# Score products of the gated attention as four 64x64 tiles, placed ahead of the preceding unit's outputs, with other PSUM banks for the outputs

## The chip, the core and the metric

The kernel runs on one core of a Trainium2 chip. TensorE (PE in the profile, PEld for its weight loads) does the matrix products and writes them to PSUM, VectorE (DVE) and ScalarE (ACT) work elementwise and read PSUM, GpSimd (POOL) works elementwise on SBUF, SyncE (SP) issues the DMA transfers. The metric is the device time of one launch in microseconds; lower is better.

## The reference, cut to what matters

Three stages run one after the other on a sequence of 4 batches x 768 steps x 384 columns: a gated linear attention of 8 heads of 48, a two-layer MLP behind a layer norm, and a token-mixing block followed by a second MLP.

```python
f = 1.0 / (1.0 + np.exp(-f_logit))
for t in range(S):                       # per batch b and head h, state is 48 x 48
    state = f[:, :, t, :, None] * state + np.einsum('bhd,bhe->bhde', k[:, :, t], v[:, :, t])
    y[:, :, t] = np.einsum('bhd,bhde->bhe', q[:, :, t], state)
...
xn = (x - mu) / np.sqrt(var + 1e-06) * g_ln
x = x + np.maximum(xn @ w_ch1, 0.0) @ w_ch2
...
u = x + (np.maximum(x.transpose(0, 2, 1) @ w_tok1, 0.0) @ w_tok2).transpose(0, 2, 1)
out = u + np.maximum(u @ w_ch1, 0.0) @ w_ch2
```

## The kernel before

**Units of attention.** The recurrence is cut into chunks of 128 steps. A unit n is one chunk of one batch with all 8 heads: 24 units, unit n being chunk n // 4 of batch n % 4. Heads lie in 4 pairs p, and the two heads r of a pair stand in two halves of the partitions (rows 0 to 47 and 64 to 111). The logarithms of the gates are summed along the chunk, and queries and keys are scaled with the exponentials, so that a chunk becomes plain products. Each step of a unit has a name, used in the order table as `unit.step`:

- `lf`, `lq`, `lv` (or `lt`, `lv` from unit 3 on): loads of the gate logits, of queries and keys, of values; from unit 3 one load `lt` brings logits, queries and keys as one tile `T` (two buffers)
- `clamp` (VectorE or GpSimd), `log` (two ScalarE activations), `scan` (VectorE), `ek` and `eq` (ScalarE exponentials), `km` and `qm` (keys and queries scaled), `tot` (GpSimd)
- `kp`, `kt`: 4 transposes of the keys on TensorE and their copy out of PSUM
- `sc` (line 318): the scores, 8 products of 48 rows x 128 columns with a stream of 128; `A0`, `A1` (line 323) mask them and copy them to SBUF
- `y`: the outputs, first state times queries (line 335, 48 rows x 64 or 48 columns; not for the first chunk), then values times scores (line 339, 128 rows x 64 or 48 columns); `yc0`, `yc1` copy them out
- `st` (line 364): keys times values, the addition to the state; `ste` adds it, `std` decays it
- `yt` (4 transposes), `lna`, `lnc`, `lnv`, `lnr` (layer norm), `tp` (3 transposes), `ah`, `al` (the normed rows split into two parts for three-product matmuls)

An fp32 product on TensorE appears in the trace as two passes, so 8 products are 16 records.

**MLP work.** Behind the attention, three units make one step of the first MLP: 12 groups `mS.f` (line 469) and 12 groups `mS.ouG` (line 499) of 9 matmuls of 384 columns each; `h`, `l`, `r` are their copies out of PSUM. `wI.ld/.a/.b/.c/.h/.l` load and convert one piece of weights for them. Token mixing and the second MLP follow.

**What sets the order.** Every step is put on a slot list. Up to slot 77 the order of all engines is the table `ORDER`, written out by hand; `name+k` puts k filler products (`busy`, line 432, bf16 zeros of 256 columns) ahead of that step's own products. 56 such products (line 572) also open the program. Behind slot 77 the order follows the slot numbers of the tuple at the end of `attention`: with `s0` the unit's base slot and 8 slots to a unit, one slot being a group of 9 MLP matmuls, `sc` stands at s0-1, `y` and `st` at s0+2, `yt` at s0+4, `kp` at s0-3, `tp` at s0+7. Engines work strictly in this order.

**PSUM.** `mmp` has 3 banks for the MLP, `scp` 2 banks that scores and outputs `yT` take in turn, `atp` 3 banks for `kp`, `y`, `st` and `tp` in turn.

The function that the change touches, with the lines that the profile names:

Of the kernel before, what the change touches and what calls it, by code (L numbers as in the profile page):

```python
# [7 lines left out]
F32 = mybir.dt.float32  # L8
# [13 lines left out]
C = 128  # L22
# [29 lines left out]
    1.tot 0.y+6 1.qm 2.log 2.lq 3.clamp 1.km 0.yc0 0.yc1 2.scan 1.kp+7 3.log 2.lv 1.sc w5.ld w2.a 2.ek
    3.scan 0.yt 2.eq w15.ld 1.kt 2.km 3.ek 1.st+8 w14.ld 1.A1 0.std 3.eq 2.kp 1.A0 0.lna 4.lt 2.qm 1.y+4
    1.ste 2.kt 0.lnc 1.yc0 3.qm 0.tp+3 1.yc1 2.st 0.ah 3.lv 3.km 1.yt 0.lnv 0.al 1.std 3.sc w1.ld 1.lna w2.b
    w4.ld 3.kp 2.ste 1.lnc 3.kt 3.A1 4.lv 4.clamp 1.tp+3 3.st 3.A0 1.ah w12.ld 0.lnr 1.lnv 1.al 3.y 4.log
    w1.a w3.ld 2.tot w1.b 3.yc0 5.lv 4.scan 3.yc1 3.ste 2.sc+9 w5.a 4.ek 3.tot 3.yt 4.eq 2.A1 3.std 5.lt
    3.lna 2.A0 4.km 2.y+7 w5.b 4.kp 2.yc0 4.qm 2.yc1 4.kt 2.yt+4 w5.c 4.sc 3.lnc 2.lna w13.ld w2.c w5.h 3.tp
    2.lnc w2.h 4.st 4.A0 5.clamp 3.ah 2.tp 3.lnv 4.A1 w2.l 2.ah 3.al 4.y+5 5.log 2.al 3.lnr 4.tot 2.lnv m0.0
    5.scan 6.lt 4.yc0 4.yc1 w3.a 5.ek 4.yt 4.ste 2.lnr m0.2 4.lna 5.km 6.lv 5.eq 4.lnc 5.kp 5.qm 4.tp 5.kt
    w3.b 5.sc 4.ah 4.lnv 4.std 4.al 5.st 5.A0 5.tot 1.lnr 5.A1 w3.c 5.y+6 6.clamp w3.h w5.l 6.log w1.c m0.5  # L60
    7.lt 5.ste w3.l 5.yc0 5.yc1 m0.h0 6.scan 5.yt m0.h2 5.lna m0.l2 5.std 7.lv m0.l0 6.ek 5.lnc m0.3+12 6.eq
# [5 lines left out]
    w17.b w17.c w11.ld w20.a w17.h m0.o20 w20.b 8.lv w17.l w6.a m0.o11 8.clamp w6.b 8.log w6.c m0.o21 w11.a
    w6.h w11.b m0.r11 w6.l 6.ste m1.o10 w11.c 8.scan w11.h m0.o01 w11.l w20.c m1.o11 7.clamp w21.ld w20.h
    m0.r01 6.std 7.log m0.r21 w22.ld w20.l m1.o00 7.scan m1.o20 w9.a 7.ek w9.b 8.ek m1.r11 7.km 7.eq m1.o01
    8.eq w9.c 8.km w7.ld w9.h 6.tp m0.6 m1.r01 6.lnv 7.tot w10.ld 8.tot 8.qm w8.ld m1.o21 7.qm 6.lnr 7.sc  # L70
    w7.a m0.h6 m1.r21 w9.l m0.l6 m1.6 w7.b w7.c 7.A1 w7.h m1.9 m1.h6 w7.l m1.l6 w10.a m1.7 w10.b m1.h9 w10.c
    m1.l9 w10.h m0.7 m1.h7 w10.l m1.l7 w22.a m1.10 w22.b m0.h7 w22.c w21.a w22.h w21.b 7.kp m1.h10 m0.11
    w22.l 7.kt w21.c 7.A0 w18.ld w21.h 7.st m0.h11 m1.l10 w21.l 7.y m0.l7 w19.ld w8.a w8.b w23.ld m0.9 w8.c
    7.yc0 9.lt 7.yc1 w18.a w8.h w18.b m0.l11 w8.l 8.sc m0.h9 7.ste w18.c m1.8 8.A1 7.std w18.h 9.lv 8.A0
    s0.ld w18.l m0.8 m1.h8 m1.l8 9.clamp m0.l9 8.y w19.a 9.log w19.b s1.ld w19.c m0.h8 m1.11 9.scan w19.h
    m0.l8 w19.l 9.ek m0.10 9.eq w23.a s2.ld m1.h11 9.qm m1.l11 m0.o22 6.ah m0.h10 w23.b 6.al 9.km m0.o12
# [78 lines left out]
def main_path(ctx, tc, qkf_t, v_n, g_rep, w1, w2, wt1, wt2, w3, w4, out, x1_d, f_d):  # L155
# [17 lines left out]
    zeros = const.tile([128, 256], BF16, name="zeros")  # L173
# [66 lines left out]
    def attention(n):  # L240
# [7 lines left out]
        def load(f, rows, name):  # L248
            def g():
                if "T" not in t:  # L250
                    if n < 3:
                        t["T"] = first[:P2, 12 * n:12 * n + 12, :].rearrange("p (j a) c -> p j a c", j=3)
                    else:
                        t["T"] = sb.tile([P2, 3, NP, C], F32, tag="T", name="T")
                nc.sync.dma_start(out=t["T"][:, rows], in_=qkf_t[n][:, rows])  # L255
            sl.e(f, g, name)
# [49 lines left out]
        def ktrans_e():  # L306
            t["kt"] = s1.tile([128, NP * P2], F32, tag="kt", name="kt")
# [63 lines left out]
        def stat_e():  # L371
            new = t["st"][:P2, :NP * D]
# [612 lines left out]
```

## Time and profile before

| | us |
|---|---|
| time before, median of 3 runs (798.78 to 801.06) | 800.78 |
| the profiled execution, its own time | 798.34 |
| the span of that execution, first to last instruction | 796.6 |
| TensorE busy | 785.7 (99%) |
| VectorE busy | 398.5 (50%) |
| ScalarE busy | 332.3 (42%) |
| GpSimd busy | 208.9 (26%) |

The rest of this document sets its sums against the profiled execution, 798.34 us, of which 1.7 us lie outside the span. Its views are read thus: the page gives shares of busy time; the chain names the work that ended last; the waits name which engine stood still for which; a timeline lists instructions of one engine with their start. TensorE overlaps its instructions, so the lengths of its records add up to more than the time that they take; what a stretch of TensorE costs is read from the starts.

### The profile page before, as it was taken

The page shows a single profiled execution, that of the slowest core. Times are in us where ns is not written, and L with a number is a line of the kernel's source. Part 1 is how long each engine was busy: PE and PEld are TensorE (multiplying, and loading weights), DVE is VectorE, ACT ScalarE, POOL GpSimd, SP SyncE. Part 2 cuts the span into 40 slices and gives each one's busy share as a digit, 9 for nine tenths or more (in the row PEclk, how much of TensorE's full clock was granted, in tenths as well). Part 3 has the DMA queues.
Part 4 walks back from the last instruction along what each step waited for, and adds up shares of the span by engine and source line. Part 5 has one row for each costly group of instructions (what it writes and reads, how often), then busy time and mean ns, then how long its engine had stood idle before and what let it go on. Part 6 is the DMA issues. An engine that isn't in the chain of part 4 may idle for free.

```text
span 796.6 us, 14109 instructions
## 1 busy us (share of the span) xinstructions
PE 785.7 (99%) x5618; PEld 758.5 (95%) x5618; DVE 398.5 (50%) x745; ACT 332.3 (42%) x841; POOL 208.9 (26%) x267
## 2 busy tenths in 40 slices
PE   9999999999999999999999999999999999999996
PEld 7799999999999999999999999999999999999996
DVE  6789895554655545555263353525344443434220
ACT  6764453443534425343253453425344444425020
POOL 2552241432423443232004451211211111111000
PEclk9999999999999999999999999999999999999999
DMA  9736353445544345441243553334333433322001
GB/s 252 226 91 199 87 161 99 126 123 158 162 118 147 110 124 175 129 153 51 77 132 90 181 153 104 88 101 130 109 78 101 125 104 104 96 90 60 31 1 34
DMA packets 42844, 93.23 MB, mean 117 GB/s; under 512 B 4800, under 2 KB 25408, under 8 KB 42768
## 3 DMA queue, kind: packets, MB, share of 16 engines
q1 hardware_dynamic: 42768, 92.23, 39.3%
q8 instruction: 46, 0.75, 0.4%
q14 instruction: 30, 0.25, 0.1%
HBM read 76.48 MB, written 15.73 MB: 116 GB/s over the span
## 4 chain that ended last, share of the span: by engine, by line
PE 93%; DMA 3%; DVE 1%; SPq 1%; ACT 1%; issue 0%; POOL 0%; DVEq 0%
PE mo L499 38%; PE mm L469 37%; PE ht L684 3%; PE rt L660 3%; PE sc L318 3%; DMA T<-in_qkf_t 3%; PE yT L339 3%; PE tp L438 2%; PE yT L335 1%; PE y L353 1%; PE st L364 1%; PE kp L303 1%; DMA xr<-x_d 1%; SPq L255 0%; POOL T L267 0%
## 5 line engine op out<-in xcount | busy, mean ns | idle before, releaser
L469 PE MATMUL mm<-ah,w1h 128*128 128x384 f32 x576 | 197.5, 343 | 0.0
L499 PE MATMUL mo<-w2h,hh 128*128 128x384 f32 x576 | 196.8, 342 | 0.0
L469 PE MATMUL mm<-ah,w1l 128*128 128x384 f32 x576 | 192.9, 335 | 0.0
L499 PE MATMUL mo<-w2h,hl 128*128 128x384 f32 x576 | 192.9, 335 | 0.0
L469 PE MATMUL mm<-al,w1h 128*128 128x384 f32 x576 | 192.6, 334 | 0.0
L499 PE MATMUL mo<-w2l,hh 128*128 128x384 f32 x576 | 192.6, 334 | 0.0
L484 ACT ACTIVATE hh<-mm 128x384 fp32r<-128x384 f32 x192 | 94.0, 490 | 206.9 <-PE mm L469 204.2
L488 DVE SCALAR_TENSOR_TENSOR hl<-mm,hh 128x384 fp32r<-128x384 f32 x192 | 106.3, 555 | 139.6 <-ACT hh L484 139.4
L469 PEld LDWEIGHTS mm<-ah,w1h 128*128 128x128 f32 x576 | 108.2, 188 | 2.2 <-issue 0.7
L499 PEld LDWEIGHTS mo<-w2h,hh 128*128 128x128 f32 x576 | 108.1, 188 | 2.0 <-issue 0.5
L469 PEld LDWEIGHTS mm<-al,w1h 128*128 128x128 f32 x576 | 108.3, 188 | 0.0
L499 PEld LDWEIGHTS mo<-w2l,hh 128*128 128x128 f32 x576 | 108.2, 188 | 0.0
L499 PEld LDWEIGHTS mo<-w2h,hl 128*128 128x128 f32 x576 | 108.1, 188 | 0.0
L469 PEld LDWEIGHTS mm<-ah,w1l 128*128 128x128 f32 x576 | 108.1, 188 | 0.0
L738 POOL TENSOR_TENSOR cs<-cs 128x384 f32<-128x384 f32 x56 | 47.4, 848 | 222.5 <-DVE cs L735 183.3
L267 POOL TENSOR_SCALAR T<-T 112x512 f32<-112x512 f32 x17 | 26.1, 1536 | 109.6 <-DMA T<-in_qkf_t 106.6
L451 ACT ACTIVATE ah<-tp 128x384 fp32r<-128x384 f32 x48 | 23.4, 487 | 69.6 <-PE tp L438 69.5
L529 DVE TENSOR_TENSOR xr<-mo,xr 128x384 f32<-128x384 f32 x24 | 13.4, 556 | 67.9 <-PE mo L499 67.9
L518 DVE SCALAR_TENSOR_TENSOR x<-mo,rs,x 128x384 f32<-128x384 f32 x30 | 18.4, 617 | 51.9 <-PE mo L499 51.8
L455 DVE TENSOR_TENSOR al<-tp,ah 128x384 fp32r<-128x384 f32 x48 | 26.4, 551 | 33.1 <-ACT ah L451 33.0
L741 ACT ACTIVATE cs<-cs 128x384 f32<-128x384 f32 x56 | 31.0, 553 | 9.4 <-POOL cs L738 9.3
L323 DVE TENSOR_TENSOR A<-sc,upper 128x512 f32<-128x512 f32 x48 | 31.0, 685 | 7.4 <-PE sc L318 7.2
(142 smaller groups left out, 1015.5 us busy)
## 6 DMA issues: line engine op xcount, KB each, us to landing
cs<-in_w SPq DMA_DIRECT2D x48, 384.0 KB, 3.3
sg<-in_w SPq DMA_DIRECT2D x44, 384.0 KB, 3.9
T<-in_qkf_t SPq DMA_DIRECT2D x21, 672.0 KB, 5.3
f_d<-cu SPq DMA_DIRECT2D x32, 192.0 KB, 1.9
wf<-f_d SPq DMA_DIRECT2D x32, 192.0 KB, 2.5
x_d<-x SPq DMA_DIRECT2D x24, 192.0 KB, 1.9
xr<-x_d SPq DMA_DIRECT2D x24, 192.0 KB, 3.4
out<-xr SPq DMA_DIRECT2D x24, 192.0 KB, 1.9
```

The lines of the kernel that those rows point to most:

```text
L267: eng("clamp").tensor_scalar(f, f, -43.0, None, op0=ALU.max)
L318: nc.tensor.matmul(t["sc"][r][:, p], t["K"][rows(r), p, :], t["Q"][rows(r), p, :])
L323: nc.vector.tensor_tensor(a, t["sc"][g], upper.rearrange("p (o c) -> p o c", o=1).to_broadcast([128, NP, 128]), op=ALU.mult)
L339: nc.tensor.matmul(t["yT"][r][o, p // 2], t["V"][:, D * h:D * h + o.stop - o.start], t["A", r][:, p, :], start=(c == 0 and p < 2), stop=(p ...
L455: nc.vector.tensor_tensor(al, src, ah.bitcast(F32), op=ALU.subtract)
L469: nc.tensor.matmul(ps, w[:, f, k, :], x[:, k, :], start=(i == 0), stop=(i == 8))
L484: nc.scalar.activation(out=hid(f)[0], in_=t[f], func=AF.Relu)
L488: nc.vector.scalar_tensor_tensor(hl, t[f], 0.0, hh.bitcast(F32), op0=ALU.max, op1=ALU.subtract)
L499: nc.tensor.matmul(ps, x, w[:, f, :], start=(f == lo and i == 0), stop=(f == hi and i == 2))
L660: nc.tensor.matmul(t["r"][j][:, :DM], w[:, s, js], t[x, s], start=(s == 0 and i == 0), stop=(s == NCH - 1 and i == 2))
L738: nc.gpsimd.tensor_tensor(t["u"], t["u"], t["h"], op=ALU.subtract)
L741: nc.scalar.activation(out=t["u"], in_=t["u"], func=AF.Abs, accum_out=wlow[:, i:i + 1])
```

## The change

- A score product is issued as two, each with 64 of the 128 key columns: 16 products of 48 rows x 64 columns instead of 8 of 48 x 128. The stream stays 128 long, the results land in the same places.
- In the slot tuple `sc` goes from s0-1 to s0-6.1, just ahead of the `y` of the unit before (s0+2 there); the steps that prepare it go earlier by 2.5 to 5 slots, and the masks `A0`, `A1` by 5.
- The outputs `yT` move from `scp` to `atp`; scores have `scp` alone. `st` has no bank of its own any more: its products go to columns 256 to 447 of the first `yT` bank, beside the outputs in columns 0 to 255.
- The load is split for all units: logits in a tile `F` of their own (s0-16), queries and keys in `T` (s0-13). `kt` has two buffers.
- Filler products have 224 columns instead of 256.
- The table `ORDER` is written anew, with other fillers (89 before, 88 now) and other steps on GpSimd.

TensorE in the middle of the attention, before (`tp` are transposes of unit 12's norm, `sc` the scores of unit 13, `mm` the MLP):

```order
L469 MATMUL mm<-ah,w1h 128x384
L469 MATMUL mm<-al,w1h 128x384
L469 MATMUL mm<-ah,w1l 128x384
L438 MATMUL tp<-ident,xn 128x128 x3
L318 MATMUL sc<-T 128x128 x8
```

and now, where `sc` are the scores of unit 14 and the `yT` rows the outputs of unit 13:

```order
L471 MATMUL mm<-ah,w1h 128x384
L471 MATMUL mm<-al,w1h 128x384
L471 MATMUL mm<-ah,w1l 128x384
L321 MATMUL sc<-T 64x128 x16
L339 MATMUL yT<-T,state_119 64x128 x2
L339 MATMUL yT<-T,state_119 48x128 x2
L339 MATMUL yT<-T,state_119 64x128 x2
L339 MATMUL yT<-T,state_119 48x128 x2
L343 MATMUL yT<-A_2599,V 64x128
```

The scores stood alone behind the transposes, with 27 MLP matmuls between them and the outputs; now the next unit's scores and this unit's outputs are one block.

SyncE's queue of loads at the start, before (`first` and `firstv` hold the first three units, 512 columns are logits, 1024 queries and keys, 1536 all three; `in_w` are weights):

```order
L547 DMA gln<-in_g_rep 128x384
L255 DMA first<-in_qkf_t 112x512
L192 DMA firstv<-in_w 128x768
L255 DMA first<-in_qkf_t 112x512
L255 DMA first<-in_qkf_t 112x1024
L255 DMA first<-in_qkf_t 112x512
L263 DMA firstv<-in_v_n 128x384
L255 DMA first<-in_qkf_t 112x1024
L255 DMA T<-in_qkf_t 112x1536
L192 DMA firstv<-in_w 128x768
```

and now:

```order
L549 DMA gln<-in_g_rep 128x384
L251 DMA first<-in_qkf_t 112x512 x2
L259 DMA first<-in_qkf_t 112x1024 x2
L266 DMA firstv<-in_v_n 128x384 x2
L251 DMA first<-in_qkf_t 112x512
L251 DMA F<-in_qkf_t 112x512
L259 DMA first<-in_qkf_t 112x1024
L266 DMA firstv<-in_v_n 128x384
L193 DMA sg<-in_w 128x768
L193 DMA firstv<-in_w 128x768
```

The first weights went from third place to behind the loads of three units.

The core of the diff (the shift of the preparing steps, and of the table a line):

```diff
-    0.lf w0.ld 1.lf 0.lq 0.clamp 0.log w0.a w0.b 2.lf 0.scan 0.lv 1.clamp 0.ek 1.lq w0.c 0.eq 0.km w0.h
+    0.lf 1.lf 1.lq 0.clamp 0.log 0.lq 1.clamp 1.log 0.scan 0.lv 1.scan 0.ek 1.lv 0.eq 2.lf 1.ek 0.tot 0.qm
...
-    zeros = const.tile([128, 256], BF16, name="zeros")
+    zeros = const.tile([128, 224], BF16, name="zeros")
...
-            t["kt"] = s1.tile([128, NP * P2], F32, tag="kt", name="kt")
+            t["kt"] = s2.tile([128, NP * P2], F32, tag="kt", name="kt")
...
-                    nc.tensor.matmul(t["sc"][r][:, p], t["K"][rows(r), p, :], t["Q"][rows(r), p, :])
+                    for s in (slice(0, 64), slice(64, 128)):
+                        nc.tensor.matmul(t["sc"][r][s, p], t["K"][rows(r), p, s], t["Q"][rows(r), p, :])
...
-            t["yT"] = [scp.tile([128, NP, 128], F32, tag="sc", name="yT") for _ in range(2)]
+            t["yT"] = [atp.tile([128, NP, 128], F32, tag="at", name="yT") for _ in range(2)]
...
-        def stat(z=0):
-            ps = atp.tile([128, 512], F32, tag="at", name="st")
-            t["st"] = ps
-            busy(ps, z)
+        def stat():
+            ps = t["st"] = t["yT"][0].rearrange("p a c -> p (a c)")[:, 256:256 + NP * D]
...
-            load(s0 - 11, slice(0, 3), f"{n}.lt")
-            sl.e(s0 - 11, load_v, f"{n}.lv")
+            lo = (s0 - 16, s0 - 13, s0 - 11)
...
-                (-9, sl.e, pre_clamp, "clamp"), (-8, sl.e, pre_log, "log"), (-7, sl.e, pre_sum, "scan"),
-                (-6, sl.e, pre_ek, "ek"), (-6, sl.e, pre_eq, "eq"), (-5, sl.e, pre_qm, "qm"),
-                (-5, sl.e, pre_km, "km"), (-5, sl.e, pre_tot, "tot"), (-3, sl.p, None if last else ktrans, "kp"),
-                (-2, sl.e, None if last else ktrans_e, "kt"), (-1, sl.p, scores, "sc"),
-                (0, sl.e, lambda: scores_e(0), "A0"), (0, sl.e, lambda: scores_e(1), "A1"),
+                (-13, sl.e, pre_clamp, "clamp"), (-12, sl.e, pre_log, "log"), (-11, sl.e, pre_sum, "scan"),
+                (-10, sl.e, pre_ek, "ek"), (-10, sl.e, pre_eq, "eq"), (-7.5, sl.e, pre_qm, "qm"),
+                (-8.5, sl.e, pre_km, "km"), (-9, sl.e, pre_tot, "tot"), (-3, sl.p, None if last else ktrans, "kp"),
+                (-2, sl.e, None if last else ktrans_e, "kt"), (-6.1, sl.p, scores, "sc"),
+                (-5, sl.e, lambda: scores_e(0), "A0"), (-5, sl.e, lambda: scores_e(1), "A1"),
...
-            nc.tensor.matmul(ps[:, :256], zeros[:, :128], zeros)
+            nc.tensor.matmul(ps[:, :224], zeros[:, :128], zeros)
```

## Rows read from the trace of the kernel before

**Rows 1.** The page: span, and each engine's busy time, share, instructions.

```profile
span 796.6 us, 14109 instructions
PE 785.7 (99%) x5618; PEld 758.5 (95%) x5618; DVE 398.5 (50%) x745; ACT 332.3 (42%) x841; POOL 208.9 (26%) x267
```

**Rows 2.** The chain that ended last: shares by line, and one late piece (start, length).

```profile
PE mo L499 38%; PE mm L469 37%; PE ht L684 3%; PE rt L660 3%; PE sc L318 3%; DMA T<-in_qkf_t 3%; PE yT L339 3%; PE tp L438 2%; PE yT L335 1%; PE y L353 1%; PE st L364 1%; PE kp L303 1%; DMA xr<-x_d 1%; SPq L255 0%; POOL T L267 0%
714.46 18.72 PE mm L469 x108
```

**Rows 3.** Waits of TensorE: waiting <- waited for: us in total, times, longest.

```profile
PE warm L572 <- DVE zeros L542: 1.1, 1, 1.1
PE sc L432 <- ACT ys L345: 1.0, 1, 1.0
PE yT L432 <- DVE A L323: 0.7, 3, 0.3
PE st L364 <- DMA V<-in_v_n: 0.4, 1, 0.4
```

**Rows 4.** Timeline of TensorE, scores between MLP matmuls: start, length, what, passes.

```profile
59.63 0.34 PE L469 MATMUL mm<-ah,w1l 128*128 128x384 f32 x1
59.90 1.16 PE L318 MATMUL sc<-T 48*128 48x128 f32 x16
60.99 0.45 PE L469 MATMUL mm<-ah,w1h 128*128 128x384 f32 x1
61.27 0.34 PE L469 MATMUL mm<-al,w1h 128*128 128x384 f32 x1
```

**Rows 5.** The same view, a block of key transposes, outputs and state products.

```profile
65.61 0.34 PE L469 MATMUL mm<-ah,w1l 128*128 128x384 f32 x1
65.78 0.55 PE L303 MATMUL kp<-ident,T 112*128 112x112 f32 x4
66.26 0.65 PE L335 MATMUL yT<-T,state 48*64 48x128 f32 x16
66.85 1.09 PE L339 MATMUL yT<-A,V 128*64 128x128 f32 x16
67.76 0.62 PE L364 MATMUL st<-V,kt 128*48 128x48 f32 x16
68.31 0.45 PE L469 MATMUL mm<-ah,w1h 128*128 128x384 f32 x1
68.60 0.34 PE L469 MATMUL mm<-al,w1h 128*128 128x384 f32 x1
```

**Rows 6.** Groups by form: weight loads of the state product, count | busy, mean ns.

```profile
L335 PEld LDWEIGHTS yT<-T,state 48*64 48x64 f32 x160 | 8.2, 132 | 4.6 <-issue 2.9 <-DVE hl L488 0.8 <-DVE cu L211 0.2
L335 PEld LDWEIGHTS yT<-T,state 48*48 48x48 f32 x160 | 7.7, 119 | 0.0
```

**Rows 7.** Timeline of TensorE at the start: opening fillers, later fillers, first MLP matmul.

```profile
1.12 8.42 PE L572 MATMUL warm<-zeros 128*128 128x256 bf16 x56 [1.12 <-DVE zeros L542]
9.38 0.82 PE L432 MATMUL kp<-zeros 128*128 128x256 bf16 x6
...
18.61 1.04 PE L432 MATMUL st<-zeros 128*128 128x256 bf16 x8
19.58 0.67 PE L364 MATMUL st<-firstv,kt 128*64 128x48 f32 x16
...
40.72 0.45 PE L469 MATMUL mm<-ah,w1h 128*128 128x384 f32 x1
```

**Rows 8.** Timeline of VectorE at the start, around the first scan.

```profile
6.71 0.36 DVE L201 TENSOR_SCALAR cu<-firstv 128x384 int32<-128x384 int32 x1 [2.27 <-DMA firstv<-in_w]
7.58 1.22 DVE L276 TENSOR_TENSOR_SCAN first<-seg,first 112x512 f32<-112x512 f32 x1
```

**Rows 9.** Busy time by stretch: PE, PEld, DVE, ACT, POOL (counts), clock, DMA.

```profile
0.00:40.70 40.70, 37.44 (x431) 29.95 (x431) 29.39 (x53) 28.30 (x66) 17.72 (x33) 1.00 0.81 234
53.10:86.90 33.80, 33.80 (x246) 32.97 (x244) 31.46 (x65) 16.63 (x37) 8.62 (x12) 1.00 0.49 144
```

**Rows 10.** Waits, all engines: the clamp for its load.

```profile
POOL T L267 <- DMA T<-in_qkf_t: 106.6, 16, 12.6
```

More of the change, by code (lines that the diff above doesn't have):

```diff
@@ L52 @@
[L52 to L61, printed above, removed]
@@ L67 @@
[L67 to L76, printed above, removed]
@@ new lines @@
+    1.eq 3.lf 0.km 2.lq 1.qm 0.kp+17 0.sc 0.kt 1.km 2.clamp 1.kp 0.A1 2.lv 2.log 3.clamp 0.A0 w5.ld 1.tot
+    1.kt 0.y+8 2.scan 3.log w0.ld 0.st 3.lq 1.sc 0.yc0 3.scan 0.ste 0.yc1 2.ek 0.yt 1.A1 0.std 2.eq 4.lf
+    2.km 0.lna w14.ld 2.qm 2.kp+8 2.kt 0.lnc 4.lq 3.ek 1.A0 2.tot 0.tp+6 0.ah w0.a 1.y 4.clamp 3.eq 0.al
+    0.lnv w15.ld 3.qm 1.st 1.yc0 2.sc w0.b w13.ld 1.yc1 1.ste 3.km 4.log 1.yt 2.A1 w4.ld 2.A0 1.std 3.kp+4
+    1.lna 3.lv 3.sc 4.scan 3.kt w3.ld 2.y 1.lnc 4.ek w1.ld 3.A1 0.lnr 1.tp 2.yc0 4.lv 2.st 4.km 1.ah 2.yc1
@@ new lines @@
+    w2.ld 1.al 3.tot 4.eq w0.c 2.ste 5.lf 4.qm w0.h 2.yt+11 1.lnv w1.a 4.kp w3.a 2.lna 3.A0 2.std 4.tot 4.kt
+    4.sc+6 2.lnc 6.lf w3.b 2.tp 4.A1 w0.l 3.y 2.ah 2.lnv 2.al 5.clamp 4.A0 3.st 5.lq 3.yc0 m0.0 3.ste w3.c
+    3.yc1 w2.a w3.h 3.std 5.log 5.lv 3.yt w3.l 4.y w2.b 3.lna 5.scan 4.st 4.yc0 6.lq 3.lnc m0.3 4.yc1 w1.b
+    5.ek 4.ste 1.lnr 5.eq 6.lv 5.km 3.tp 4.yt 3.ah 5.qm 5.kp 4.lna w1.c 5.sc 3.al 5.kt 5.tot 4.lnc 7.lf w1.h
+    3.lnv 5.A1 4.std 4.tp+4 5.A0 w1.l 4.ah 4.lnv 4.al 5.y+6 w14.a w2.c 6.clamp m0.h0 w15.a 5.st 5.yc0 7.lq
@@ new lines @@
+    m1.h4 w17.a w16.h w17.b m1.l4 w16.l m0.o00 w17.c w7.a w17.h m0.o10 w17.l w7.b m0.o21 w7.c w10.a w6.ld
+    w7.h w7.l m0.o01 w8.ld m0.r21 6.scan w19.ld m0.o11 m0.r01 6.ek w6.a 6.eq w6.b m1.o00 6.qm m0.r11 w6.c
+    m1.o10 w8.a w6.h w8.b w6.l m1.o01 w8.c 6.km w8.h m1.o20 m1.r01 6.tot 8.lf w8.l w10.b 6.kp m1.o21 w10.c
+    6.kt 7.scan w11.ld w10.h 6.sc w23.ld m1.r21 8.clamp 7.ek 7.eq m1.o11 w18.ld 6.A1 7.km 8.log 6.A0 w9.ld
+    w10.l 7.kp m1.r11 7.tot m0.6 7.kt 9.lf 8.scan w18.a 8.ek m1.10 w18.b 8.eq w18.c m0.h6 7.qm m0.7 w18.h
@@ new lines @@
+    w20.b m0.l9 8.sc w20.c m1.h9 6.al w20.h m1.l9 s3.ld 7.y w20.l 8.A1 8.A0 m0.o22 10.clamp 9.lq 7.yc0
+    9.scan 7.yc1 10.log m0.o12 w21.a 9.ek w21.b w21.c 9.eq s0.a w21.h m0.o02 9.tot 9.km 11.lf w21.l 9.kp
+    s1.a m0.o03 9.qm m0.o13 m0.r03 s1.b m0.d0 s1.c m0.o23 m0.r13 s0.b m0.d1 s0.c 7.st m0.r23 s0.h 9.sc 9.kt
+    7.ste 10.scan 9.lv 8.y m0.d2 9.A1 7.std 10.ek 9.A0 10.eq 10.lq 8.st 10.tot m1.o12 8.ste 8.std 10.lv 7.yt
+    m1.o22 7.lna 8.yc0 10.km 8.yc1 m1.o13 7.lnc 10.qm 8.yt m1.r13 7.tp 8.lna m1.o02 m1.d1 7.ah 8.lnc 7.lnv
@@ L246, in eng, with load_f, load_q @@
             return nc.gpsimd if n >= P["NV"] or f"{n}.{x}" in POOL else nc.vector
[L248 to L256, printed above, removed]
+        def load_f():
+            t["F"] = first[:P2, 12 * n + 8:12 * n + 12, :] if n < 3 else sb.tile([P2, NP, C], F32, tag="F", name="F")
+            nc.sync.dma_start(out=t["F"], in_=qkf_t[n][:, 2])
+        def load_q():
+            if n < 3:
+                q = first[:P2, 12 * n:12 * n + 8, :].rearrange("p (j a) c -> p j a c", j=2)
+            else:
+                q = sb.tile([P2, 2, NP, C], F32, tag="T", name="T")
+            t["Q"], t["K"] = q[:, 0], q[:, 1]
+            nc.sync.dma_start(out=q, in_=qkf_t[n][:, 0:2])
         def load_v():
@@ L371, in stat_e @@
         def stat_e():
-            new = t["st"][:P2, :NP * D]
+            new = t["st"][:P2]
             if c:
@@ L571, in warm @@
         for _ in range(k):
[L572 removed]
+            nc.tensor.matmul(wt[0][:, :224], zeros[:, :128], zeros)
     sl.p(0.1, lambda: warm(P["WARM0"]))
```

46 lines of the change are left out of this document (23 added, 23 removed).

## The prediction

> **What bounds the kernel now.** First the page's busy times and the chain. TensorE is busy 785.7 of 796.6 us, every other engine half of the span or less [rows 1], and the chain is TensorE nearly throughout: MLP products 75%, scores 3%, outputs 3 + 1% [rows 2]. Then the waits of TensorE: 1.1 us at the very start, 1.0, 0.7 and 0.4 us later [rows 3], the last of these before the MLP runs steadily. So the time is the sum of TensorE's own work, and an edit counts by what it takes out of that sum; work saved elsewhere counts only at the start, where TensorE is kept going with fillers. Then the timelines, for the price of a block. A stretch of 108 MLP matmuls lasts 18.72 us [rows 2], 0.173 each. What a block between MLP matmuls costs is the time from the last matmul ahead of it to the second behind it, less two times 0.173: for scores alone 61.27 - 59.63 - 0.35 = 1.29 us [rows 4]; for key transposes, outputs and state products together 68.60 - 65.61 - 0.35 = 2.64 us [rows 5].
>
> **Reading the blocks.** The transposes take 66.26 - 65.78 = 0.48 until the state product starts, 0.10 of it the pause that scores show too (59.63 + 0.17 to 59.90) [rows 4, 5], so 0.39 is theirs and 2.25 is left for outputs and state products. A unit thus pays 1.29 + 2.25 = 3.54 us for scores, outputs and state products, in two blocks, and the transposes 0.4 a block. The scores use the array in two halves by rows: 16 passes in 8 rounds of two, 60.99 - 59.90 = 1.09 us with the pause at the end. The state product, 48 rows x 64 columns, is the row nearest to the new scores: 16 passes in 66.85 - 66.26 = 0.59 us, pause included [rows 5]. With four passes at a time that is 4 rounds. The values product behind it takes 8 rounds of two without a pause at its end: 0.91 us, 0.114 a round.
>
> **The scores (the largest term).** Split, they are 32 passes instead of 16, in four quarters: 8 rounds again. The split by itself gains nothing; alone between MLP matmuls the new scores cost about what the old ones do. The gain is the place. Directly ahead of the state product, which has the same tile shape, they need no pause between them and no entry and exit of their own: the block grows by 8 rounds and the 1.29 us go. Price of a round: 0.114 by the values product; 0.125 by the difference of old scores and state product (1.09 - 0.59 over 4 rounds). I take 0.114, the row without a pause in it: 0.91 us. Per unit 1.29 - 0.91 = 0.38 saved, 0.29 by the other price. By the order of the changed kernel 16 of the 24 units have their scores directly ahead of a preceding unit's outputs behind the first MLP matmul (unit 8 on); one more has them so ahead of it, units 5 to 7 stand apart and stay as they were. 16 x 0.38 = **-6.1 us** (bounds -4.6 and, if a round is 0.1, -7.8). All of it lies on the path, since TensorE doesn't wait there.
>
> **The start.** The first MLP matmul comes at 40.72 us [rows 7]; of the 39.6 us from the first filler on, the opening fillers take 9.38 - 1.12 = 8.26, 71 later fillers 0.97 / 8 = 0.121 each, 8.6, waits 2.0 [rows 3, 7] and so attention blocks 20.7. The new order has one unit fewer ahead of the first MLP matmul: 2.25 + 0.4 + 0.3 (outputs and state, one block of 4 and one of 3 transposes) move behind it, 2.95. One score block there loses its pauses: 20.7 - 2.95 - 0.4 = 17.3. Fillers, an estimate from these rows by their columns: 56 at 224 / 256 of 8.26, 7.2, and 60 at 0.106, 6.4 (bounds: unchanged per filler, 8.26 and 7.3). That is 1.1 + 7.2 + 6.4 + 17.3 = 32.0 us plus waits. Can the data be there? The first scan stands at 7.58 behind two steps of weights, for which VectorE waited 2.27 us [rows 8]; with these loads and steps moved back it needs only the logarithms, which follow the clamp, and that chain starts nearly 2 us earlier. VectorE has 39 steps ahead of the first MLP matmul instead of 46, some 3.3 us less by their mean times, 26 of its 29.4 us [rows 9]. 26 in 33.5 is 78%, against 72% now and 93% between 53 and 87 us, where TensorE never waited [rows 9]. So I put waits at 1.5 us (before: 2.0; bounds 0, and 8.7, which is no gain at all): first MLP matmul at 33.5, 7.2 earlier, less the 2.95 moved: **-4.3 us** (bounds -5.8 to +3).
>
> **Behind it.** 28 fillers at 0.106 instead of 18 at 0.121 and 0.3 of small waits between them: 3.0 against 2.5, **+0.5**. Another **+0.5** for waits of the new order there that no row shows: VectorE's work up to the second half of the first MLP step is the same with TensorE some 8 us earlier, but below the 93%.
>
> **Edits that I cost at nothing, and what hides them.** The outputs' new banks: `atp` now carries five tiles a unit (two of outputs, two of transposes, one of the norm) on three banks; the key transposes take over the first outputs' bank after 27 MLP matmuls, 4.7 us, while two output copies and the state addition need about 1 us. Without that cover each unit would pay up to 1 us. The state products in the outputs' bank: at worst `yc0` must wait until they end, 0.55 us later [rows 5], covered by 18 MLP matmuls (3.1 us) ahead of the `yt` transposes; at the start, where that cover is short, up to 4 x 0.55, within the waits above. The masks wait for scores in another place of VectorE's queue, and behind them stand the copies of MLP results; since the scores now open a block of over 3 us, these run while TensorE is still in it. The loads: logits come 3 slots ahead of their clamp instead of 2, good for a clamp that waits for its load in 16 units [rows 10]; queries and keys come 6.9 slots ahead of the scores instead of 10, and their buffer is free only once the outputs two units back are done. A slot is 1.56 us of matmuls and its share of blocks, so 6.9 are over 12 us for a load, two scalings and queueing. 21 more DMA issues stand on SyncE, which has room; ahead of them in its queue are weights that aren't due for long.
>
> **The sum.** -6.1 - 4.3 + 0.5 + 0.5 = -9.4 us. The profiled execution took 798.34, so it would take 788.9; the median of the runs is 2.4 above that execution, and from it the sum gives 791.4. I write 791.
>
> **Rivals.** First, the start doesn't shorten: what was filler becomes wait, since the chain of one unit (scores, mask, outputs, copy, transposes, norm) is as long as before. For it: fillers were there because TensorE waits for data, and a shorter filler brings no data. Against it: weights leave that chain. The 4.3 us go: -5.1, about 795.5. Second, the change doesn't do what it says: a pause stays between scores and state product, or scores wait for the scaled queries, whose lead is shorter. For it: clamps already wait for their loads [rows 10]. The 6.1 us go: -3.3, about 797.5; both together leave it where it is, about 801. Third, slower: the four quarters don't load their weights together, and the two that share rows take turns. One score load of 64 columns takes 0.132 us [rows 6]; 16 for each half of the rows in turn are 2.1 us in place of 0.91, +1.2 in 24 units, +28.8 - 9.4, about 820; it decides from 0.4 us a unit, a third of that. Against it: the state product's 16 loads, 8 of 0.132 and 8 of 0.119, 2.0 us together, lie in 0.59 us [rows 5, 6], where turns within each half of the rows would need 1.0.
>
> This third way is also a rule: the Trainium skill ("TensorE: Matmul & The Clock Gate", Part 3, "The mechanism") says that a weight load overlaps running matmuls only when its row group differs. By that rule the sum would be the third rival's; the rows of the state product speak against it, so I give it little.
>
> **How the numbers follow.** Forecast 0.62, start not shortened 0.20, no gain from the block 0.07, both 0.06, loads in turn 0.05. The forecast's own range is 787 (round at 0.1, no waits) to 794; the first two rivals reach to 797, and 786.5 to 797 leaves out about 0.2. A measurement of this kernel can tell about 0.3%, 2.4 us, from no change. Faster by more than that: 0.62 + 0.20 + half of the second rival, 0.86; the same 0.08; slower 0.06.
>
> **What would show it.** In the changed kernel's timeline, 32 passes of scores directly ahead of the state product, the start of one to the start of the other 0.9 to 1.0 us, and a block with state products at 3.1 to 3.2 us where 2.25 stands now; the first MLP matmul at 32 to 35 us; waits of TensorE under 4 us in all. The prediction is wrong if that start is near 40, if TensorE waits for GpSimd or a load at the scores, or if scores take 1.5 us or more.

## The result and the profile after

The changed kernel takes 792.3 us (median; 790.29 to 795.12) against 799.74 (798.78 to 801.06) before: a ratio of 0.9907, interval 0.9881 to 0.9932, or 7.4 us less. On another occasion it took 791.23 against 799.95, ratio 0.9896, interval 0.9876 to 0.9916. The forecast was 791, faster, with a range from 786.5 to 797: direction and time held. The profiled execution took 792.3 us with a span of 790.6; before, 798.34 and 796.6 [rows 1].

The page of the profile after: span, busy time of each engine (share, instructions), and the chain that ended last, by engine and by line (the lines here are those of the changed kernel: scores L321, state product L339, values product L343, state update L366).

```profile
span 790.6 us, 14897 instructions
PE 777.5 (98%) x6001; PEld 756.2 (96%) x6001; DVE 403.9 (51%) x742; ACT 328.8 (42%) x841; POOL 209.6 (27%) x270
PE 90%; DMA 4%; DVE 1%; ACT 1%; POOL 1%; SPq 1%; issue 1%; POOLq 0%; DVEq 0%
```

TensorE has 8.2 us less work and 777.5 of 790.6 us busy; it is still the bound. The 4% of DMA in the chain are for the most part these pieces of it (start, us, what; in order of time), one in the opening and two that end in waits of the first MLP steps:

```profile
4.77 9.53 DMA F<-in_qkf_t
...
99.38 5.00 DMA T<-in_qkf_t
113.63 4.78 DMA T<-in_qkf_t
```

TensorE's waits in the changed kernel, the list that answers to [rows 3]: releaser, us in total, times, longest.

```profile
PE kp L305 <- DVE first L291: 1.8, 2, 1.4
PE sc L321 <- DVE A L326: 1.1, 1, 1.1
PE warm L574 <- DVE zeros L544: 1.1, 1, 1.1
PE kp L305 <- POOL T L291: 1.0, 2, 0.7
PE tp L440 <- DVE xn L394: 0.7, 1, 0.7
```

Without the first filler's these rows are 4.6 us, more than the 4 that the prediction allowed for all waits. The first row holds the 1.44 us of unit 0's keys, the second is a mask that stands behind two weight conversions in VectorE's queue. Next, TensorE's timeline around one block far from the start (start, us, line, operation, count); it answers to [rows 4] and [rows 5].

```profile
138.18 0.34 PE L501 MATMUL mo<-w2h,hl 128*128 128x384 f32 x1
138.45 1.10 PE L321 MATMUL sc<-T 48*64 48x128 f32 x32
139.37 0.62 PE L339 MATMUL yT<-T,state 48*64 48x128 f32 x16
139.92 1.09 PE L343 MATMUL yT<-A,V 128*64 128x128 f32 x16
140.83 0.62 PE L366 MATMUL yT<-V,kt 128*48 128x48 f32 x16
141.38 0.44 PE L501 MATMUL mo<-w2h,hh 128*128 128x384 f32 x1
141.66 0.34 PE L501 MATMUL mo<-w2l,hh 128*128 128x384 f32 x1
```

The 32 quarter passes stand directly ahead of the state product: 139.37 - 138.45 = 0.92 us from the start of one to the start of the other, where the prediction had worked out 0.91. The whole block costs 141.66 - 138.18 - 0.35 = 3.13 us; before, the same products cost 1.29 + 2.25 = 3.54 in two blocks [rows 4, 5]. Eleven units have this block at 3.13, one has it behind another piece, and four, without state update, have 2.69 in place of 3.09.

And the opening, which answers to [rows 7] and [rows 8]: TensorE's first rows, two of those with a wait in them and the first MLP matmul; then VectorE's first scaling of queries.

```profile
1.10 8.10 PE L574 MATMUL warm<-zeros 128*128 128x224 bf16 x56 [1.10 <-DVE zeros L544]
9.04 1.79 PE L434 MATMUL kp<-zeros 128*128 128x224 bf16 x17
12.27 0.57 PE L305 MATMUL kp<-ident,first 112*128 112x112 f32 x4 [1.44 <-DVE first L291]
...
25.27 0.60 PE L305 MATMUL kp<-ident,T 112*128 112x112 f32 x4 [0.33 <-POOL T L291]
...
36.27 0.44 PE L471 MATMUL mm<-ah,w1h 128*128 128x384 f32 x1
```

```profile
10.88 0.69 DVE L294 TENSOR_TENSOR first<-first,eq 112x512 f32<-112x512 f32 x1 [2.00 <-DMA first<-in_qkf_t]
```

The first MLP matmul is at 36.27, not at 33.5. Unit 0's queries are scaled at 10.88, after 2.00 us of waiting for their load; its key transposes, the first work of TensorE that isn't filler, wait 1.44 us behind that.

### The profile page after: what moved, and what is told of

Its sections match the earlier page's. It is cut to its first block, busy times and chain, and to the rows that moved or that the text cites. A ratio compares the mean times of both kernels' runs of the same rounds, so it can differ in the third digit from the quotient of the medians.

```text
span 790.6 us, 14897 instructions
## 1 busy us (share of the span) xinstructions
PE 777.5 (98%) x6001; PEld 756.2 (96%) x6001; DVE 403.9 (51%) x742; ACT 328.8 (42%) x841; POOL 209.6 (27%) x270
## 4 chain that ended last, share of the span: by engine, by line
PE 90%; DMA 4%; DVE 1%; ACT 1%; POOL 1%; SPq 1%; issue 1%; POOLq 0%; DVEq 0%
PE mo L501 38%; PE mm L471 35%; PE ht L686 3%; PE rt L662 3%; PE sc L321 3%; PE yT L343 3%; PE tp L440 2%; DMA T<-in_qkf_t 1%; DMA F<-in_qkf_t 1%; PE yT L339 1%; DMA wf<-f_d 1%; PE yT L366 1%; PE y L357 1%; PE kp L305 1%; DMA xr<-x_d 0%
## 5 line engine op out<-in xcount | busy, mean ns | idle before, releaser
L349 ACT ACTIVATE ys<-yT 112x256 f32<-112x256 f32 x48 | 16.8, 382 | 74.9 <-PE yT L366 55.8
L270 POOL TENSOR_SCALAR F<-F 112x512 f32<-112x512 f32 x19 | 29.9, 1574 | 21.5 <-DMA F<-in_qkf_t 21.5
```

## The experiments

**The scores whole again, in the new place (e1_whole).**

```diff
-                    for s in (slice(0, 64), slice(64, 128)):
-                        nc.tensor.matmul(t["sc"][r][s, p], t["K"][rows(r), p, s], t["Q"][rows(r), p, :])
+                    nc.tensor.matmul(t["sc"][r][:, p], t["K"][rows(r), p, :], t["Q"][rows(r), p, :])
```

> The changed kernel with each head pair's scores as one product over all 128 columns again, in the new place and with the outputs in the other banks. The changed kernel's block of scores, state product, values product and state update costs 3.13 us beyond the MLP matmuls around it. Theory (the gain is that the quarters, half as wide in the array, run side by side with the products behind them, without the pause at a change of tile shape): 3.3 to 3.4 us, over 16 units +3.5 to +4.5 us, total 796 to 797. Rival (the place alone is the gain, one block in place of two): 3.13 as now, total 792. Second rival (the quarters' passes are themselves cheaper): more than 3.5, total 798 or above.

TensorE's timeline of the same block:

```profile
136.56 1.16 PE L320 MATMUL sc<-T 48*128 48x128 f32 x16
137.65 0.65 PE L338 MATMUL yT<-T,state 48*64 48x128 f32 x16
138.23 1.09 PE L342 MATMUL yT<-A,V 128*64 128x128 f32 x16
139.15 0.62 PE L365 MATMUL yT<-V,kt 128*48 128x48 f32 x16
139.70 0.44 PE L500 MATMUL mo<-w2h,hh 128*128 128x384 f32 x1
```

From scores to state product 137.65 - 136.56 = 1.09 instead of 0.92, and the block costs 3.34 instead of 3.13: the pause at the change of tile shape is there again, 0.2 us as the theory said. The total is 793.86 us (ratio 0.9925, 0.9894 to 0.9957), 1.6 to 2.6 us over the two medians of the changed kernel and less than the theory's 796 to 797. The 16 units by 0.21 are 3.4 us; of these 2.6 are left from the first to the last MLP matmul (750.16 us where the changed kernel's profile has 747.55), since the waits of two transposes were 0.7 shorter in this run. The blocks decide for the theory; by the total alone, the intervals overlap.

**The split alone (e2_split_only):** the same edit the other way, on the kernel before.

> The kernel before with the scores in quarters and nothing else: old place, old banks. Theory (a block of scores alone between MLP matmuls goes from 1.29 to 1.23 us, as one such block in the changed kernel shows): -0.06 x 16 = -1 us, total 798 to 800. Rival (the quarters are the gain wherever they stand): -0.4 us for each of the 16 units, total 793.

The scores alone between MLP matmuls go from 1.29 to 1.23 us in all their places, as in these rows (95.51 - 93.93 - 0.35):

```profile
93.93 0.34 PE L500 MATMUL mo<-w2h,hl 128*128 128x384 f32 x1
94.20 1.10 PE L319 MATMUL sc<-T 48*64 48x128 f32 x32
...
95.51 0.34 PE L470 MATMUL mm<-al,w1h 128*128 128x384 f32 x1
```

799.42 us, ratio 0.9985 (0.997 to 1.0001): in quarters but in the old place the scores gain next to nothing.

**The scores apart again (e3_apart).**

```diff
-                (-2, sl.e, None if last else ktrans_e, "kt"), (-6.1, sl.p, scores, "sc"),
+                (-2, sl.e, None if last else ktrans_e, "kt"), (-7.1 if n > 10 else -6.1, sl.p, scores, "sc"),
```

> The changed kernel with the scores of units 11 to 23 (13 units) one MLP group earlier, so that they again stand alone between MLP matmuls. Theory (one block less is the gain): scores alone 1.23, the outputs' block back to about 2.25, sum 3.5 where 3.13 stands; +0.35 to +0.4 x 13 = +4.5 to +5.2 us, total 797. Rival (the place is worth nothing, the outputs' banks and the opening carry the gain): total 792 to 793.

The 13 units moved pay 1.23 for scores alone and 2.25 for the rest (1.80 in the three without state update), 3.48, as forecast. 796.58 us, ratio 0.9947 (0.9932 to 0.9963). These three runs and the kernel before fill a table of one block's price in us:

| | scores alone, outputs later | scores directly ahead of the outputs |
|---|---|---|
| whole | 1.29 + 2.25 = 3.54 (before) | 3.34 (e1_whole) |
| in quarters | 1.23 + 2.25 = 3.48 (e2, e3) | 3.13 (changed kernel) |

The place alone takes off 0.20, the split alone 0.06, both together 0.41. So the gain is one pause less for the place, and 0.15 more that the split brings only where the state product, of the same tile shape, comes next.

**The outputs in the old banks (e4_old_banks).**

```diff
-            t["yT"] = [atp.tile([128, NP, 128], F32, tag="at", name="yT") for _ in range(2)]
+            t["yT"] = [scp.tile([128, NP, 128], F32, tag="sc", name="yT") if n >= 10 else
+                       atp.tile([128, NP, 128], F32, tag="at", name="yT") for _ in range(2)]
...
-                (-5, sl.e, lambda: scores_e(0), "A0"), (-5, sl.e, lambda: scores_e(1), "A1"),
+                (-5.1 if n > 10 else -5, sl.e, lambda: scores_e(0), "A0"),
+                (-5.1 if n > 10 else -5, sl.e, lambda: scores_e(1), "A1"),
```

> The changed kernel with the outputs of units 10 to 23 back in the two banks that the scores use; the scores stay directly ahead, so the outputs' products wait until VectorE has masked the scores of their own banks. Theory: two masks of 0.68 us stand between scores and state product, so each block gets an idle time of 1.2 to 1.5 us on TensorE, over 13 to 14 units +16 to +20 us, total 808 to 813. Rival (the masks come early enough, the banks don't matter): total 792 to 794.

One line of TensorE's waits, two blocks of its timeline, and two stretches at the first of them (busy us and counts of PE, PEld, DVE, ACT, POOL; then the granted clock, the share of the DMA engines and GB/s):

```profile
PE yT L340 <- DVE A L326: 13.6, 26, 1.2
```

```profile
156.37 1.10 PE L321 MATMUL sc<-T 48*64 48x128 f32 x32
158.68 0.43 PE L340 MATMUL yT<-T,state 48*64 48x128 f32 x2 [1.21 <-DVE A L326]
159.27 0.65 PE L340 MATMUL yT<-T,state 48*64 48x128 f32 x14 [0.17 <-DVE A L326]
159.85 1.84 PE L344 MATMUL yT<-A,V 128*64 128x128 f32 x16
...
178.64 0.43 PE L340 MATMUL yT<-T,state 48*64 48x128 f32 x2 [0.78 <-DVE A L326]
179.24 0.65 PE L340 MATMUL yT<-T,state 48*64 48x128 f32 x14 [0.17 <-DVE A L326]
```

```profile
159.00:162.00 3.00, 2.83 (x44) 2.56 (x44) 0.22 (x1) 0.00 (x0) 0.00 (x0) 0.67 0.31 44
163.50:167.00 3.50, 3.50 (x23) 3.47 (x23) 0.69 (x2) 2.19 (x5) 0.43 (x1) 1.00 0.61 191
```

816.76 us, ratio 1.0194 (1.0158 to 1.023): without the other banks the new place would have cost 16 us over the kernel before instead of gaining 7. The waits for the masks are 13.6 us in 26 pieces. The blocks grew by more, 24.8 us: most by 1.6, of which the two waits are 0.95 and the rest stands in new pauses around them; two by 2.0; and two by 3.0 and 3.35, where behind the wait TensorE was granted 0.67 and 0.69 of its clock over 3 us (the values product took 1.84 in the first, instead of 1.09). The theory's sum, 16 to 20, counted the idle times alone and was too small.

**Unit 0's own load first (e5_own_first).**

```diff
-    0.lf 1.lf 1.lq 0.clamp 0.log 0.lq 1.clamp
+    0.lf 1.lf 0.lq 0.clamp 0.log 1.lq 1.clamp
```

> The changed kernel with unit 0's load of queries and keys issued ahead of unit 1's. In the changed kernel TensorE waits 1.44 us at 12.27 for unit 0's scaled keys, behind scaled queries that stood 2.00 us for that load; the first MLP matmul is at 36.27. Theory (the load's place in the queue makes the wait, but a later wait for the load of unit 4 at 25.27 takes most of it back): the wait at 12.27 falls under 0.4, the one at 25.27 grows by about 1, first MLP matmul 35.5 to 36.3, total 791.5 to 792.3. Rival (nothing takes it back): first MLP matmul 34.9, total 790.9. Second rival (the load isn't the cause): nothing moves.

The wait at unit 0's keys falls from 1.44 to 0.42 and the transposes come at 10.47. But unit 0's values product now waits 1.42 us for its mask, where 0.18 stood, unit 3's keys are at 25.17 (25.27) and the first MLP matmul at 36.16 (36.27). 791.25 us, ratio 0.9885 (0.9863 to 0.9906): no gain that can be told from the changed kernel. The 1 us gained at the first transposes was taken back, and sooner than the theory named.

**Two transposes one step later (e6_later).**

```diff
-    w9.l 6.tp 8.kt 7.sc m1.l7
+    w9.l 8.kt 7.sc 6.tp m1.l7
...
-    w21.l 9.kp s1.a m0.o03 9.qm
+    w21.l s1.a m0.o03 9.kp 9.qm
```

> The changed kernel with two transposes of TensorE's order each one step later: unit 9's keys behind the next MLP step and unit 6's normalised outputs behind unit 7's scores. In the changed kernel they wait 0.70 us each, for a multiply of GpSimd and for a VectorE instruction that ran 1.64 in place of 0.61. Theory: both idle times go, -0.9 to -1.4 us behind the start, total 791. Rival (the step behind is late by the same, since what they wait for is late): the blocks at 105.7 and 119.1 keep their sum of 4.2 us, total 792.3.

Both idle times go: the blocks cost 2.18 and 0.40 instead of 2.87 and 1.31. Yet a wait of 0.4 us for a converted weight comes up in their place, and the 746.63 us from the first to the last MLP matmul, 0.9 less than in the changed kernel's first profile, are no less than the 746.60 of its second (below). 791.47 us, ratio 0.9889 (0.9865 to 0.9912): no gain shown.

**Unit 3's mask ahead of two conversions (e7_mask_first), and all three edits (e8_best).**

```diff
-    1.lnv w1.a 4.kp w3.a 2.lna 3.A0 2.std
+    1.lnv 3.A0 w1.a 4.kp w3.a 2.lna 2.std
```

> The changed kernel with unit 3's first mask ahead of two weight conversions on VectorE. In the changed kernel unit 4's scores wait 1.12 us at 33.30 for that mask, which stood behind the two conversions (31.19 to 32.65, one of them stretched beside a GpSimd instruction). Theory: this wait goes, first MLP matmul 35.1 to 35.6, total 791.2 to 791.7. Rival (another input of the same block is as late): the wait moves to the next step and the first MLP matmul stays at 36.2.

> The three edits together: unit 0's own load first, unit 3's mask ahead of the conversions, the two transposes one step later. Theory (waits in the opening add up along one chain): first MLP matmul 34.3 to 35.2, two idle times of 0.7 gone, total 789.0 to 790.5, ratio to the kernel before 0.986 to 0.988. Rival (each wait removed uncovers the next): total 791.5 to 792.3.

e7_mask_first takes 788.94 us, ratio 0.9861 (0.9838 to 0.9885); unit 4's scores no longer wait, but the transposes behind them (of unit 2's norm) do, 0.77 us, so that 0.35 of the 1.12 us of waiting is gone: in part the theory, in part the rival. First MLP matmul: 34.05, over 1 us earlier than the theory had it, more than this edit's part. e8_best takes 790.12 us, ratio 0.986 (0.9837 to 0.9883), in the theory's range; its first MLP matmul is at 35.6, later than the theory's 34.3 to 35.2.

**The order of the loads (e9_two, e10_loads, e11_late4) and the changed kernel once more (e12_again).** e9_two is the mask and the two transposes together; the others add to it:

```diff
(e10_loads, against e9_two)
-    3.clamp 0.A0 w5.ld 1.tot
+    3.clamp 0.A0 1.tot
-    w0.b w13.ld 1.yc1
+    w0.b 1.yc1
-    w2.ld 1.al
+    w2.ld w5.ld w13.ld 1.al
(e11_late4, against e9_two)
-    2.eq 4.lf 2.km 0.lna w14.ld 2.qm
+    2.eq w14.ld w15.ld 4.lf 2.km 0.lna 2.qm
-    0.lnv w15.ld 3.qm
+    0.lnv 3.qm
```

> Unit 3's mask ahead of the conversions and the two transposes one step later, without the edit on unit 0's load. Theory (both edits keep their gains beside each other; the third edit only moved a wait): first MLP matmul 33.8 to 35.0, 746.2 to 746.8 us from there to the last MLP matmul where the changed kernel takes 747.55, total 788.0 to 789.5. Rival (the edits share one gain): total 790 or above.

> The same with two weight loads of 0.39 MB issued behind the others of the opening, where they stood ahead of unit 4's decays (one) and of four further weight loads (both). In the opening the DMA engines are busy over 95% from 4 to 28 us in every trace so far. Theory (the opening is bound by the order of its loads): unit 4's decays land about 1.6 us sooner, what is left of the wait of unit 3's keys goes, first MLP matmul 0.3 to 1.5 us before that of the run without this edit, total 787.0 to 788.5. Rival (TensorE's own work sets the opening): no difference, within 0.3 us and the spread of the loads.

> The same as the run with two edits, but with two further weight loads of 0.39 MB issued ahead of unit 4's decays, no byte more in all. Theory (loads set the opening): unit 4's decays land 3.2 us later, unit 3's keys wait 2 to 3.3 us more for the clamp's place on GpSimd behind them, first MLP matmul 36.0 to 38.0, total +2 to +3.3 over the run with two edits, 790.5 to 792.5. Rival (TensorE's own work sets the opening): 0 to +0.5.

> The changed kernel itself once more, on the chip of the three runs above. Theory: its opening differs from run to run with the rate of the loads alone (first MLP matmul between 34.5 and 37.5 where unit 0's queries and keys land between 8.6 and 10.0), and from the first MLP matmul on it takes 747.2 to 747.9 us again; total 791 to 793. Rival (the opening is the same each time): first MLP matmul within 0.3 of 36.27.

| | us (ratio to before, interval) | wait of unit 3's keys | first MLP matmul |
|---|---|---|---|
| e9_two | 789.28 (0.9863, 0.9844 to 0.9882) | 1.32 | 36.36 |
| e10_loads | 790.67 (0.9891, 0.9866 to 0.9916) | none | 36.66 |
| e11_late4 | 793.37 (0.9919, 0.9897 to 0.994) | 2.99 | 39.99 |
| e12_again | 791.23 (0.9896, 0.9876 to 0.9916) | none | 34.13 |

Two weight loads more ahead of unit 4's decays (the gates' logits, `F`) cost 4.1 us, with the same work and the same bytes: more than the theory's 2 to 3.3, and against the rival. Two fewer take the wait away, as expected, but bring no gain in time: e10_loads missed its 787.0 to 788.5. e9_two kept to its total (788.0 to 789.5), not to its opening (33.8 to 35.0). e12_again kept to its total; its opening, 34.13, and its 746.60 us from the first to the last MLP matmul were both less than expected (34.5 to 37.5 and 747.2 to 747.9). The stretches of TensorE tell a part of both (busy us, count, granted clock, DMA share, GB/s), first of e10_loads, then of e11_late4:

```profile
12.00:16.00 4.00, 3.03 (x44) 0.81 1.04 249
16.00:20.00 4.00, 4.00 (x71) 0.77 1.04 263
```

```profile
28.00:32.00 4.00, 3.90 (x50) 0.57 0.63 235
```

e10_loads waited 3.20 us for unit 0's keys in its profile, and the clock then granted was 0.81 and 0.77; e11_late4 fell to 0.57 behind its wait of 2.99. Whether e10_loads would gain at the rate of loads that e12_again had stays open.

e12_again is the same program as the changed kernel, and its profile comes near the one that the prediction described. Its rows at the start, of TensorE and then of VectorE:

```profile
1.10 6.84 PE L574 MATMUL warm<-zeros 128*128 128x224 bf16 x56 [1.10 <-DVE zeros L544]
10.77 0.57 PE L305 MATMUL kp<-ident,first 112*128 112x112 f32 x4 [1.20 <-issue]
34.13 0.44 PE L471 MATMUL mm<-ah,w1h 128*128 128x384 f32 x1
```

```profile
9.38 0.69 DVE L294 TENSOR_TENSOR first<-first,eq 112x512 f32<-112x512 f32 x1 [0.74 <-DMA first<-in_qkf_t]
```

In ten profiles the same program runs up to here (e5 and e8 load in another order and are left out; e10 issues one weight load less at about 9 us; e1 differs in the scores behind it). The starts of unit 0's first scaling, of its key transposes, and of the first MLP matmul:

| | scaled queries | key transposes | first MLP matmul |
|---|---|---|---|
| e12_again | 9.38 | 10.77 | 34.13 |
| e1_whole | 9.56 | 10.95 | 34.56 |
| e7_mask_first | 9.86 | 11.25 | 34.05 |
| e6_later | 9.90 | 11.29 | 35.92 |
| changed kernel | 10.88 | 12.27 | 36.27 |
| e4_old_banks | 11.03 | 12.42 | 37.48 |
| e11_late4 | 11.06 | 12.46 | 39.99 |
| e3_apart | 11.27 | 12.67 | 39.81 |
| e9_two | 11.30 | 12.69 | 36.36 |
| e10_loads | 11.58 | 12.97 | 36.66 |

The transposes follow the scaling by 1.39 or 1.40 us each time, whether the opening fillers ended at 7.9 or 9.5: when the load lands decides, and it differs by up to 2.2 us from run to run. The first MLP matmul doesn't follow these two columns (e10_loads is last in them and not in the third). e3_apart and e11_late4 are latest, in part because the clock fell behind waits of 1.68 and 2.99 us (0.57 granted over 4 us).

## Why the prediction was right, and where it was wrong

Two profiles of the changed kernel against the one of before, by the terms of the sum (us; the blocks are the difference of their prices over the 16 units, the start is the first MLP matmul less the 2.95 of moved work, the third row is what is left between first and last MLP matmul):

| term | forecast | first profile | e12_again |
|---|---|---|---|
| scores' blocks, 16 units | -6.1 | -6.5 | -6.4 |
| start | -4.3 | -1.5 | -3.6 |
| fillers and waits behind it | +1.0 | +2.7 | +1.6 |
| behind the last MLP matmul | 0 | -0.7 | -0.9 |
| sum (span) | -9.4 | -6.0 | -9.3 |

**The blocks: right, with their working.** 0.91 us forecast for the quarter passes, 0.92 measured; 0.38 a unit forecast, 0.41 measured. The mechanism was shown from both sides (e1_whole, e3_apart): a pause goes with the place, and more with the split in that place. That the split by itself gains nothing was forecast and is what e2_split_only shows, but for 0.06. The third rival, loads of quarters in turn, would need 2.1 us where 0.92 stand, and fell, as the state product's rows had said [rows 5, 6]. The Trainium skill's rule that a weight load overlaps running matmuls only with another row group ("TensorE: Matmul & The Clock Gate", Part 3, "The mechanism") doesn't hold for these quarters, two of which share their rows: the measurement decides.

**Edits costed at nothing: right for the banks.** The outputs and state products in three shared banks show no wait in the list above. What these banks save was not priced; e4_old_banks shows that it is the condition of the whole change, 25 us.

**The start: the step that failed.** Its later fillers and blocks were sized right: 36.27 - 1.10 - 7.94 - 3.47 of waits = 23.8 us, where the prediction had 6.4 + 17.3 = 23.7. Two items were off: the opening fillers (7.94 for 7.2) and above all the waits (3.5 for 1.5); in e12_again these were 6.68 and 2.7. With 224 columns the opening fillers took 6.68 to 8.26 us in the profiles, and with 256, before, 8.26: the moment at which they speed up (last section) weighs more than their columns. For the waits the prediction asked "Can the data be there?" and answered with VectorE's share of busy time, 78%. That share came out lower, 74% (26.7 of 36.27 us), and the waits came all the same, so it was the wrong measure. Up to unit 0's first scaling VectorE had time and waited for loads; from 12 to 28 us it was busy for 14.8 of 16 us, and one of the waits, 1.12 us, is for a mask in its own queue, behind two weight conversions of which the first waited 0.61 us for its load. That loads set the pace stood in the chain of the kernel before, in two pieces that the prediction passed over:

```profile
4.69 10.76 DMA T<-in_qkf_t
15.46 11.01 DMA T<-in_qkf_t
```

From 4.69 to 26.47 us what the chain went through was transfers, no engine. The DMA engines' share in the first 40 us had been in the rows, 0.81 at 234 GB/s [rows 9], and from 8 to 28 us it is 0.98 or more in every profile, that of before too. In the new order unit 1's queries and keys stand ahead of unit 0's in SyncE's queue, so that unit 0's scaled queries start between 9.38 and 11.58 and the fillers, which were to end near 10, end before the data is there.

That is the first wait, but not the load that set the first MLP matmul: with unit 0's load first (e5_own_first) it came only 0.11 us earlier. The chain of the changed kernel goes through the logits `F` of unit 3 (4.77 to 14.30 us; 4.68 to 12.55 in e12_again). In the first profile it then goes through GpSimd, where the clamp of unit 4's logits waits for its load and unit 3's keys are scaled behind it:

```profile
22.43 1.49 POOL L270 TENSOR_SCALAR F<-F 112x512 f32<-112x512 f32 x1 [2.74 <-DMA F<-in_qkf_t]
23.89 1.33 POOL L291 TENSOR_TENSOR T<-T,ek 112x512 f32<-112x512 f32 x1
```

Unit 3's key transposes follow at 25.27 (23.06 in e12_again), and from these to the first MLP matmul both profiles, e4, e5 and e6 take 11.0 to 11.1 us. e11_late4, which delayed unit 4's logits, moved the transposes to 28.10, where e9_two had them at 26.45. That a better order of loads would gain is not shown: e5 and e10 gained nothing. Nor did any run take back one edit of the start by itself (the narrower fillers, the weights moved back, the logits' own tile), so what each is worth stays open.

The first rival ("a shorter filler brings no data") had the mechanism and 0.20; of its 4.3 us, 2.8 came true in the first profile and 0.7 in e12_again.

**Behind the start:** +1.0 forecast, +2.7 and +1.6 found. The fillers' 0.5 is counted in each. Of the rest, 1.8 in the first profile (1.1 in e12_again) are those of two transposes at 105.7 and 119.1 us, each behind a slow VectorE or GpSimd instruction and these behind loads of queries and keys whose buffer came free late. The prediction held the loads of the later units for covered ("over 12 us"); unit 8's landed 0.6 us late and unit 9's 0.3. Taking the two transposes out of that cost nothing and gained nothing (e6_later).

**The 0.7 to 0.9 us behind the last MLP matmul** were not forecast, and their cause stays open.

So the median, 791.2 to 792.3, came out within 1.3 us of the forecast, with 0.3 to 0.4 us more gained in the blocks than forecast and 1.3 to 4.5 us less in the start and the waits behind it. How close it came is in part luck: the 0.7 to 0.9 us that nobody forecast cover some of what the start lacks, and the 791 was counted from a median before of 800.78, where the kernel before took 799.74 and 799.95 beside the changed one. The gain itself, forecast as 9.4 us, is 7.4 and 8.7 by the medians.

**Perhaps a better version:** three kernels with unit 3's mask ahead of the conversions (e7, e8, e9) have the lowest medians, 788.94, 790.12 and 789.28 (ratios 0.986 with intervals from 0.9837 to 0.9885), against 0.9896 and 0.9907 for the change as it was. But e10_loads and e11_late4 have the mask there too, with other orders of loads, and take 790.67 and 793.37. e7_mask_first is faster than the kernel before by 1.4%; over the changed kernel it is 2.3 to 3.4 us by medians that were not taken side by side, with intervals that still touch. The wait that the edit shortens accounts for 0.35 of them in e7 and 0.73 in e9. So a gain over the changed kernel is likely and not shown.

## What to carry to other kernels

When a block of small products stands between large matmuls, price its pauses: put products of the same tile shape side by side, and first find the bank that lets the second start before the first has been read. For a start that runs on fillers, follow the chain back to its first loads, and ask what stands ahead of them and how busy the DMA engines are; the share of a compute engine did not tell it here. Take a second profile of the same program before explaining 2 us of an opening.

## What the hardware showed that was not expected

**The rate of loads differs from run to run.** From 8 to 12 us the DMA engines were busy throughout and moved 238 GB/s in the first profile, 267 in e12_again and 282 in e1_whole, and unit 0's queries came up to 2.2 us apart. In the four of the ten profiles with 266 GB/s or more in that stretch they were scaled before 10 us, in the six with 259 or less at 10.88 or later. Why the rate differs, no run shows. Times of one program on one chip went from 789.13 to 793.59.

**The opening fillers speed up at a different moment in each run.** From start to start each of the 56 fillers takes 0.187 us at first and 0.096 later, half as long, as between the levels of 1.2 and 2.4 GHz, though the granted clock reads 1.00 in both stretches. In e12_again the step comes at 3.8 us, in the first profile at 6.4, in e6_later at 7.0: the same 56 products take 6.68, 7.94 and 8.26 us.

**A wait in the opening can cost the clock as well.** A stretch of e3_apart behind waits of 1.31, 0.26 and 1.68 us (columns as above), and the values product in it:

```profile
36.00:40.00 4.00, 4.00 (x48) 0.57 0.05 17
```

```profile
37.15 1.97 PE L343 MATMUL yT<-A,V 128*64 128x128 f32 x16
```

0.57 is a mixture of the levels 1.2 and 2.4 GHz; 1.97 us for what takes 1.09 is the lower one.

**VectorE is stretched beside GpSimd.** Rows of VectorE and GpSimd in the changed kernel: the norm's product alone and beside GpSimd's scaling of queries, and a weight step alone and beside its scaling of keys.

```profile
51.35 0.62 DVE L394 SCALAR_TENSOR_TENSOR xn<-x,nm,gln 128x384 f32<-128x384 f32 x1
104.51 2.19 POOL L294 TENSOR_TENSOR T<-T,eq 112x512 f32<-112x512 f32 x1 [0.53 <-DMA T<-in_qkf_t]
105.48 1.64 DVE L394 SCALAR_TENSOR_TENSOR xn<-x,nm,gln 128x384 f32<-128x384 f32 x1
117.16 0.35 DVE L202 TENSOR_SCALAR cu<-sg 128x384 int32<-128x384 int32 x1
118.56 1.56 POOL L291 TENSOR_TENSOR T<-T,ek 112x512 f32<-112x512 f32 x1 [0.33 <-DMA T<-in_qkf_t]
118.90 1.43 DVE L202 TENSOR_SCALAR cu<-sg 128x384 int32<-128x384 int32 x1
```

0.62 became 1.64, and 0.35 became 1.43; the masks, which read PSUM, took 0.68 wherever they stood. The Trainium skill ("SBUF — State Buffer", "Who interferes with whom") says that VectorE instructions with two SBUF inputs, or in a two-port mode, share a port pair with GpSimd, and that whoever issues first blocks the other. The norm's product, with two inputs in SBUF and issued 1 us behind the GpSimd instruction, agrees with it; whether the weight step ran in such a mode no row shows, and no run here moved the GpSimd work away to test it.
